# First transform of a long convolution by channel halves of one sequence

## Chip, core and metric

The kernel runs on one core of a Trainium2 chip. The core has a matrix engine (PE, TensorE), whose weight loads are shown apart (PEld), a vector engine (DVE), a scalar engine (ACT), GpSimd (POOL) and a queue engine (SP); each works through its own instructions in order and waits for the others by semaphores. The metric is the device time of one execution in microseconds; of several executions the median is taken.

## What is computed

The input is x (8 sequences of 5696 positions and 128 channels), a filter h (5696 positions, 128 channels), 64 pairs of mixing matrices and one channel matrix. The reference, cut to what matters:

```python
# long convolution, position-wise causal
Xf = np.fft.rfft(x, n=2 * S, axis=1)
Hf = np.fft.rfft(h, n=2 * S, axis=0)
x = np.fft.irfft(Xf * Hf[None], n=2 * S, axis=1)[:, :S, :]
# spectral mixing of the lowest 64 modes
X = np.fft.rfft(x, axis=1)
Yr = einsum('bmd,mde->bme', Xr, w_r) - einsum('bmd,mde->bme', Xi, w_i)
Yi = einsum('bmd,mde->bme', Xr, w_i) + einsum('bmd,mde->bme', Xi, w_r)
u = x + np.fft.irfft(Y, n=S, axis=1)
out = u + np.maximum(u @ w_ch, 0.0)
```

## The kernel before

A position is written as 64 q + p, with q from 0 to 88 and p from 0 to 63. The long transform is done in two steps by matrix products. The *first transform* runs over q: for one channel, PE takes the 89 rows of x as weights (two sequences of 64 positions p make 128 columns) and a table F of cosines and sines as the moving operand, 180 columns: 90 frequencies k, real and imaginary. The result has 128 partitions (sequence, p). The *second transform* runs over p with twiddle matrices M: for each k, two parts r and two sequences b, a matmul that is 64 rows deep over 128 channels, into two PSUM banks, one for each sequence.

The eight sequences are worked in four pairs. For each pair the stages are:

- *First transform*, 32 tiles of four channels (`a_tile`): four matmuls into two PSUM banks, then one evacuation of 720 columns to the buffer As (lines 477 to 479), by ACT or DVE. In the first pair a string `SHARE` says which; each tile waits for all eight pieces of x of both sequences (`XIN`).
- *Second transform* in 23 ticks of four frequencies (`tick`, `second`). Each tick's result is copied from PSUM by ACT (Xs) or taken from PSUM by DVE, multiplied with the filter's spectrum Hs on DVE (U, line 652), transformed by PE with two matrices (`Wc`), evacuated by ACT (Zs), written to a scratch tensor, and reduced to 64 modes (`modes`, PSUM bank 7). Tick 0 is special: its matmuls are cut by channels (`DA`, `DF`: 116 or 120, then the rest), so that the first part can run before the last tiles are evacuated; it has three products (`first_u`, line 623).

The last stage (from line 773 on) mixes the modes, transforms back and writes the output. The change leaves its instructions alone, apart from where some of its buffers lie.

*The opening.* All DMA requests on x go through POOL's queue, which casts to 16 bits on the way: first h (six requests), then x of the first pair into the buffer Xr (14 requests: for each quarter c of the positions `first_rows` of both sequences, `next_rows` for both together, and `last_row`), then the twiddle table M (six). Meanwhile PE runs 92 filler matmuls. Then h has its own first transform, 16 tiles, each of four matmuls and four fillers, evacuated by ACT except for two tiles. Between them, after every second tile, DVE copies one of the eight pieces of x (89 partitions, 2048 elements) to its place in the buffer Xin (`x_place`, line 365), in which each channel's step is 130 elements. Then PE runs 22 long fillers (`LONG`), and the 32 tiles of the first pair follow, with six *filter ticks* (`filter_tick`: the second transform of h, evacuated to Hs, then swapped between partition halves by two DMAs on SP) after tiles 11, 14, 17, 20, 23 and 26. The other filter ticks run in the second transform of the first pair, six ticks ahead of their use.

*The next pair's x* is requested on POOL's queue: for the second pair four pieces (buffers Xh, which lie in the part of Hs that is filled last, and where Xr lies before) right after the eight copies, and the other pieces in the ticks. DVE copies the pieces to Xin during the ticks named in `XPLACE`.

PSUM has eight banks. The tiles of the first pair and the filter ticks take turns at four slots of two banks (`FOUR`); the tiles of h at three.

A recorder keeps the order in which instructions are written down for each engine and adds the waits from the names of what is read and written (`("xin", i)`, `("as", j)`, `("h", t, 0)`, ...). Thus the order in the program is the order on each engine.

## Time and profile before

| | us |
|---|---|
| median of three runs | 371.91 |
| lowest, highest | 370.37, 372.64 |
| span of the profiled execution, first to last instruction | 370.1 |

The profiled execution's time outside its span is not given. Its granted PE clock was 0.999 of full speed over the whole span. Busy time by stretch, in microseconds of each stretch:

| stretch | what runs | PE | DVE | ACT | share of the DMA engines |
|---|---|---|---|---|---|
| 13.0 to 23.0 | first transform of h | 9.71 of 10 | 6.01 | 8.24 | 1.07 |
| 27.3 to 43.3 | first transform, first pair | 15.44 of 16 | 14.02 | 14.45 | 1.04 |
| 49.4 to 74.6 | second transform, first pair | 25.19 of 25.2 | 24.86 | 24.02 | 1.00 |
| 74.6 to 95.0 | its end, start of the next pair | 20.40 of 20.4 | 17.09 | 19.97 | 0.73 |

A matmul's end is modelled by the profiler, so PE looks busier than it is; a share of the DMA engines over 1 comes from transfers that overlap on one engine. In the profile, As is the result of the first transform, Ah that of h, F the table, Xin the placed x, Xr, Xh and Xt the pieces as they arrive, and L323 the one line by which all matmuls are issued (L320 all DMA requests; L311, L313, L315 and L317 all evacuations).

### The profile page before, as it was taken

The page shows a single profiled execution, that of the slowest core. Times are in us where ns is not written, and L with a number is a line of the kernel's source. Part 1 is how long each engine was busy: PE and PEld are TensorE (multiplying, and loading weights), DVE is VectorE, ACT ScalarE, POOL GpSimd, SP SyncE. Part 2 cuts the span into 40 slices and gives each one's busy share as a digit, 9 for nine tenths or more (in the row PEclk, how much of TensorE's full clock was granted, in tenths as well). Part 3 has the DMA queues.
Part 4 walks back from the last instruction along what each step waited for, and adds up shares of the span by engine and source line. Part 5 has one row for each costly group of instructions (what it writes and reads, how often), then busy time and mean ns, then how long its engine had stood idle before and what let it go on. Part 6 is the DMA issues. An engine that isn't in the chain of part 4 may idle for free.

```text
span 370.1 us, 12455 instructions
## 1 busy us (share of the span) xinstructions
PE 354.7 (96%) x5350; PEld 276.5 (75%) x5350; DVE 291.8 (79%) x332; ACT 316.2 (85%) x499; POOL 75.2 (20%) x117
## 2 busy tenths in 40 slices
PE   7999899999999999999999999999999999999994
PEld 7878766667866668866668766668899888888873
DVE  3549899988999999989999988775357777756666
ACT  8559999999999999999999999995467777688885
POOL 8804012100833311823213001151000000000000
PEclk9999999999999999999999999999999999999999
DMA  7999979969999996999996999999999999999878
GB/s 139 209 271 382 249 165 292 232 198 283 93 140 213 263 258 186 132 160 215 263 278 128 171 310 363 342 345 388 381 410 386 413 410 408 418 399 376 326 291 349
DMA packets 87048, 103.94 MB, mean 281 GB/s; under 512 B 22730, under 2 KB 72522, under 8 KB 83438
## 3 DMA queue, kind: packets, MB, share of 16 engines
q1 hardware_dynamic: 64610, 81.33, 62.5%
q0 software_dynamic: 22384, 21.83, 35.4%
q8 instruction: 42, 0.69, 0.7%
q14 instruction: 12, 0.10, 0.1%
HBM read 70.61 MB, written 51.12 MB: 329 GB/s over the span
## 4 chain that ended last, share of the span: by engine, by line
PE 78%; ACT 10%; DMA 7%; DVE 3%; issue 1%; POOL 1%; DVEq 0%; POOLq 0%
PE ps L323 78%; ACT As L313 6%; DMA out_dram<-O 5%; DMA Hin<-in_h_dram 2%; ACT R L898 1%; DVE As L317 1%; ACT Xs L311 1%; DVE U L623 1%; POOL Hin L320 1%; ACT UT L311 1%; DVE O L899 0%; ACT Zs L311 0%; DVE Hp L438 0%; ACT C L313 0%; DVE Hs L315 0%
## 5 line engine op out<-in xcount | busy, mean ns | idle before, releaser
L652 DVE TENSOR_TENSOR U<-Xs,Hs 128x2048 f16<-128x2048 f16 (+1 forms) x72 | 85.8, 1197 | 12.1 <-ACT Xs L311 11.5
L323 PE MATMUL ps<-U,Wc 128*128 128x512 f16 (+1 forms) x368 | 93.8, 376 | 1.4 <-DVE U L623 1.4
L311 ACT CAST Xs<-ps 128x1024 f16<-128x1024 f32 (+1 forms) x76 | 75.0, 995 | 5.8 <-PE ps L323 3.1
L311 ACT CAST Zs<-ps 128x512 f16<-128x512 f32 (+1 forms) x132 | 70.1, 605 | 0.7
L899 DVE TENSOR_TENSOR O<-ps,R 128x512 f32<-128x512 f32 x81 | 52.4, 684 | 21.6 <-ACT R L898 11.4
L898 ACT ACTIVATE R<-ps 128x512 f32<-128x512 f32 (+1 forms) x92 | 50.5, 592 | 8.5 <-PE ps L323 8.4
L317 DVE TENSOR_SCALAR As<-ps 128x720 f16<-128x720 f32 x64 | 53.1, 879 | 4.8 <-PE ps L323 3.3
L323 PE MATMUL ps<-As,M 64*128 64x128 f16 (+3 forms) x1504 | 52.5, 214 | 2.4 <-ACT As L313 1.2
L313 ACT ACTIVATE As<-ps 128x720 f16<-128x720 f32 (+1 forms) x68 | 48.2, 771 | 5.0 <-PE ps L323 4.8
L323 PE MATMUL ps<-F,Xin 128*128 128x180 f16 x512 | 52.1, 249 | 0.1
L323 PE MATMUL ps<-WI,UT 128*128 128x256 f16 x360 | 50.8, 278 | 0.5 <-ACT UT L311 0.4
L311 ACT CAST UT<-ps 128x712 f16<-128x712 f32 x46 | 34.5, 752 | 19.4 <-PE ps L323 18.4
L323 PEld LDWEIGHTS ps<-U,Wc 128*128 128x128 f16 x368 | 29.1, 97 | 28.2 <-DVE U L623 1.9
L323 PEld LDWEIGHTS ps<-F,Xin 128*128 128x128 f16 x512 | 45.2, 155 | 6.7 <-DVE Xin L365 0.9
L323 PEld LDWEIGHTS ps<-As,M 64*128 64x128 f16 x1504 | 42.2, 94 | 8.7 <-ACT Xs L311 1.9
L323 PEld LDWEIGHTS ps<-WI,UT 128*128 128x128 f16 x360 | 38.9, 152 | 3.2 <-issue 1.8
L323 PE MATMUL ps<-IBs,C 128*128 128x356 f16 x128 | 39.2, 314 | 0.8 <-DVE O L899 0.7
L320 POOL DMA_DIRECT2D Xt<-in_x_dram x40 | 21.4, 540 | 76.5 <-PE ps L323 76.0
L323 PEld LDWEIGHTS ps<-G,Zs 128*128 128x128 f16 x512 | 26.1, 96 | 14.1 <-ACT Zs L311 0.2
L652 DVE TENSOR_TENSOR U<-ps,Hs 128x2048 f16<-128x2048 f32 (+1 forms) x16 | 35.5, 2216 | 0.0
L323 PE MATMUL ps<-G,Zs 128*128 128x128 f16 (+2 forms) x512 | 31.9, 192 | 0.1
L311 ACT CAST Zt<-ps 128x512 f16<-128x512 f32 x52 | 29.1, 659 | 0.0
(76 smaller groups left out, 479.4 us busy)
## 6 DMA issues: line engine op xcount, KB each, us to landing
out_dram<-O SPq DMA_DIRECT2D x39, 512.0 KB, 10.5
zscr<-Zs SPq DMA_DIRECT2D x62, 256.0 KB, 6.7
zscr<-Zt SPq DMA_DIRECT2D x26, 256.0 KB, 6.6
Xt<-in_x_dram POOLq DMA_DIRECT2D x20, 320.0 KB, 6.9
W<-wscr SPq DMA_DIRECT2D x4, 1024.0 KB, 8.5
ZT0a<-zscr SPq DMA_DIRECT2D x4, 1024.0 KB, 11.0
M<-cM POOLq DMA_DIRECT2D x5, 720.0 KB, 17.6
ZT1a<-zscr SPq DMA_DIRECT2D x3, 1024.0 KB, 11.1
```

Source lines behind the costliest of these rows:

```text
L311: R.add(e, lambda h_: h_.copy(dst, src), reads, writes, after=after)
L313: R.add(e, lambda h_: h_.activation(dst, src, COPY, scale=scale), reads, writes, after=after)
L317: R.add(e, lambda h_: h_.tensor_scalar_mul(dst, src, scale), reads, writes, after=after)
L320: R.add(eng, lambda h_: h_.dma_start(dst, src), reads, writes, ring=ring, after=after)
L323: R.add("tensor", lambda h_: h_.matmul(o, l, r, start=st, stop=sp), reads, writes)
L623: R.add("vector", lambda e: e.tensor_tensor(bass.AP(u_s[0], b * 512 + d0, [[2048, P], [1024, 2], [D, n], [1, d1 - d0]]), bass.AP(s_[0], s_ ...
L652: R.add("vector", lambda e: e.tensor_tensor(uv, src, hv, MULT), bk + [("h", t, 0), ("h", t, 1, 0), ("h", t, 1, J)], [("u", i)])
L898: R.add("scalar", lambda e: e.activation(rv, src_r, RELU), bk, [("r", i % NR)], after=once(("r", i % NR), G_ALL + XTT + [("y", 0), ("y", 1 ...
L899: R.add("vector", lambda e: e.tensor_tensor(ov, src_u, rv, ADD), bk + [("r", i % NR)], [key + (h_,)], after=once(key, old))
```

## The change

- *Zero columns.* The sine columns of frequencies 0 and 89 are zero. They are left out: F has 178 columns (`NF`), every evacuation of a tile 712 instead of 720, and the second transform has one part instead of two for these two frequencies, in x and in h.
- *Channel halves of one sequence.* Xin is laid out by sequence and channel half. The weights of one matmul in the first transform are two channel halves (d and d + 64) of one sequence instead of one channel of two sequences. Tiles 0 to 15 belong to sequence 0 and 16 to 31 to sequence 1. In the first pair a tile waits only for the pieces of sequence 0, or from tile 16 on for those of sequence 1 as well. In the second transform the partition halves are channel halves, and 128 columns hold 64 channels of each of the two sequences. The layouts of Hs, U and Xs follow.
- *Tick 0* is cut by sequence: `second` for sequence 0 before the tick (it needs tiles 0 to 15), for sequence 1 in it, in banks of its own (4 and 5), with 64 columns each; two products instead of three.
- *The opening.* Requests of x go sequence by sequence, 12 instead of 14. In the transform of h only the four pieces of sequence 0 are copied, after every fourth tile; DVE evacuates six tiles instead of two; two fillers a tile instead of four, and four long ones instead of 22. The four pieces of sequence 1 are copied among the tiles of the first pair, after tiles 1 and 5 by GpSimd, after 8 and 11 by DVE. The filter ticks stand after tiles 19, 21, 23, 25, 27 and 29. The second pair's four first pieces are requested after tiles 18, 20, 23 and 26, once these are evacuated.
- `modes` waits for both evacuations of a tick's Zs, since each holds a channel half.

```diff
+    NF = 2 * NK - 2
-    f1 = np.zeros((P, 2 * NK))
+    f1 = np.zeros((P, NF))
...
-    def x_place(i, src, toks):
-        R.add("vector", lambda e: e.tensor_copy(bass.AP(x_sb, i * XN * XS, [[XW, NQ], [XS, XN], [1, D]]),
+    def x_place(i, src, toks, eng="vector"):
+        R.add(eng, lambda e: e.tensor_copy(bass.AP(x_sb, i // XC * 2 * XH + i % XC * XN * HS, [[XW, NQ], [HS, XN], [XH, 2], [1, DH]]),
                                                 src),
               list(toks) + XZ, [("xin", i)])
...
+    for b_ in range(2):
+        for c_ in range(XC):
+            first_rows(b_, c_)
+            if c_ == 0:
+                next_rows(b_)
+                last_row(b_)
...
-    ZSLOT, DA, DF = 6, 116, 120
+    ZSLOT = (6, 4)
...
-    WARM, LONG = 92, 22
+    WARM, LONG = 92, 4
...
-        for i in range(4 if j < 15 else 0):
+        for i in range(2 if j < 15 else 0):
...
-             eng="vector" if j in (3, 7) else "scalar")
-        if j % 2:
-            i = j // 2 % 2 * XC + j // 4
+             eng="vector" if j in (2, 4, 6, 9, 11, 14) else "scalar")
+        if j % 4 == 3:
+            i = j // 4
...
-    def a_tile(j, slots, eng=None):
+    def a_tile(j, slots, eng=None, first_pair=False):
+        b_ = j // 16
+        xin = XIN[b_ * XC:b_ * XC + XC] if first_pair else XIN
...
-               ap(x_sb, XW, 0, P, d, [[XS, 2 * J]]), f1_sb[:, :], True, True,
-               XIN + XZ + [("f1",)], [bank(t + i // 2)])
+               ap(x_sb, XW, 0, P, d // DH * 2 * XH + d % DH, [[HS, 2 * J]]), f1_sb[:, :], True, True,
+               xin + XZ + [("f1",)], [bank(t + i // 2)])
...
+    def second(g_, t, bs=(0, 1)):
+        sl = slot_of(g_, t) if t else ZSLOT[bs[0]]
+        rd = [("as", j) for j in range(16 * bs[0], 16 * bs[-1] + 16)] + [("as", 32)] * (bs[-1] == 1)
...
+            product(g_, t, (ps, sl[0], 4096), bk[0], (0,))
+            second(g_, 0, (1,))
+            evac(bass.AP(x_s[e], 256, [[1024, P], [512, 2], [1, n]]), pv(ZSLOT[1], 256, [[512, 2], [1, n]]), bk[1], [("xs", e)], eng="scalar")
+            product(g_, t, (x_s[e], 0, 1024), [("xs", e)], (1,))
...
-    for i in range(NXH):
-        x_load(1, i, x_h[i], xtok(i), [t_ for r_ in XR for t_ in r_])
+    XTICK = [1, 5, 8, 11]
+    XNEXT = [18, 20, 23, 26]
+    HTICK = [19, 21, 23, 25, 27, 29]
     for j in range(32):
-        a_tile(j, FOUR, "both" if j == 31 else SHARE[j])
-        if j >= 11 and j % 3 == 2 and (j - 11) // 3 < LH:
+        a_tile(j, FOUR, "both" if j == 31 else SHARE[j], True)
+        if j in HTICK:
             h_ = turns("s", FOUR)
-            filter_tick((j - 11) // 3, [h_, h_ + 1])
-    second(0, 0, 0, DF)
+            filter_tick(HTICK.index(j), [h_, h_ + 1])
+        if j in XNEXT:
+            e = XNEXT.index(j)
+            x_load(1, e, x_h[e], xtok(e), [("as", j)] + [t_ for r_ in XR for t_ in r_])
+        if j in XTICK:
+            i = XC + XTICK.index(j)
+            x_place(i, bass.AP(x_all, i * XB, [[RA, NQ], [D, XN], [DH, 2], [1, DH]]), XR[i], "gpsimd" if i < XC + 2 else V)
+    second(0, 0, (0,))
```

More of the change, by code (lines that the diff above doesn't have):

```diff
@@ L493, in filter_tick @@
         for i, k in enumerate(ticks[t]):
-            for r in range(2):
+            sk = slots(k)
+            for n_, slot in enumerate(sk):
+                r = (slot + 1) % 2 if k else 0
                 for dh in range(2):
@@ L508, in filter_tick @@
         for p0, p1 in ((0, J), (J, 0)):
[L509 to L511 removed]
+            dma("sync", bass.AP(h_sb, p0 * 2 * HW + lo + 2 * w, [[2 * HW, J], [1, 2 * w]]),
+                bass.AP(h_sb, p1 * 2 * HW + lo, [[2 * HW, J], [1, 2 * w]]), "s", [("h", t, 0)], [("h", t, 1, p0)])
+        if t in GTICK:
+            q_ = GTICK.index(t)
+            s0, s1 = q_ * GP, min(q_ * GP + GP, NS)
             dma("sync", g_sb[:, s0 * P:s1 * P], bass.AP(c_g, s0 * P, [[GW, P], [1, (s1 - s0) * P]]), "c", (),
[L513 removed]
+                [("g", q_)], after=[("ag", k) for k in range(s0, s1)])
     def load_w(i):
@@ L580, in bass_long_conv_fft__then__afno_spectral_mix_kernel @@
     LC, LM, LH = 2, 3, 6
+    GTICK = [2 * i + 1 for i in range(NG)]
     ZR = 96
@@ L602, in slot_of @@
     def slot_of(g_, t):
-        if t == 0:
-            return ZSLOT
         if g_ == 0:
@@ L621, in first_u @@
-    def first_u(b, s_, row, tok, d0, d1):
-        n = len(ticks[0])
-        R.add("vector", lambda e: e.tensor_tensor(
-            bass.AP(u_s[0], b * 512 + d0, [[2048, P], [1024, 2], [D, n], [1, d1 - d0]]),
-            bass.AP(s_[0], s_[1] + d0, [[row, P], [0, 2], [D, n], [1, d1 - d0]]),
-            bass.AP(h_sb, d0, [[2 * HW, P], [HW, 2], [D, n], [1, d1 - d0]]), MULT),
-              [tok, ("h", 0, 0), ("h", 0, 1, 0), ("h", 0, 1, J)], [("u", 0)])
+            sk = slots(k)
+            for n_, slot in enumerate(sk):
+                r = (slot + 1) % 2 if k else 0
+                for dh in range(2):
+                    col = k * 3 * J + (J if r == 0 else 0) + dh * J
+                    mm(pv(sl + dh, bs[0] * 256 + i * DH, [[256, nb], [1, DH]]),
+                       ap(m_sb, MW, J * dh, J, col, [[1, P]]),
+                       ap(a_sb, AW, J * dh, J, slot * D + bs[0] * DH, [[1, nb * DH]]), n_ == 0, n_ == len(sk) - 1,
+                       rd + mtok(k), [bank(sl + dh)])
```

148 lines of the change are left out of this document (61 added, 87 removed).

## The prediction

> **What bounds the kernel now.** I read the page first, then the chain of waits in order of time, then the timeline of the opening and of one change of pair, engine by engine. Columns of chain and timeline: start, length (us), engine, line, what is written from what, count, idle time before it.
>
> ```profile
> span 370.1 us, 12455 instructions
> PE 354.7 (96%) x5350; PEld 276.5 (75%) x5350; DVE 291.8 (79%) x332; ACT 316.2 (85%) x499; POOL 75.2 (20%) x117
> PE 78%; ACT 10%; DMA 7%; DVE 3%; issue 1%; POOL 1%; DVEq 0%; POOLq 0%
> ```
> ```profile
> 4.12 7.83 DMA Hin<-in_h_dram
> ...
> 13.27 3.96 PE ps L323 x48
> ...
> 45.72 3.61 PE ps L323 x63
> ...
> 49.37 25.23 PE ps L323 x529
> ...
> 95.26 7.47 ACT As L313 x11
> 102.73 0.05 issue
> 102.78 0.37 PE ps L323 x8
> ```
>
> The long middle pieces (49.37 and after) are PE without a gap, and the change leaves their matmuls as they are, but for four short ones (64 rows deep) in each pair. So its place is elsewhere: the opening, to about 43 us, and the three changes of pair, where ACT's evacuations of As end last and a short chain follows before PE runs on. The 96% says nothing here: part of PE's busy time in the opening is filler.
>
> ```profile
> 4.65 7.51 POOL L320 DMA_DIRECT2D Xr<-in_x_dram  x14
> 11.98 2.37 DVE L438 COPY Hp<-Hin 89x4096 f16<-89x4096 f16 x2 [6.71 <-DMA Hin<-in_h_dram]
> 12.12 1.21 POOL L320 DMA_DIRECT2D M<-cM  x1
> 13.84 2.10 ACT L313 ACTIVATE Ah<-ps 128x720 f16<-128x720 f32 x3 [4.00 <-PE ps L323]
> 15.69 0.69 DVE L365 COPY Xin<-Xr 89x2048 f16<-89x2048 f16 x1 [1.34 <-DMA Xr<-in_x_dram]
> 16.30 0.90 DVE L317 TENSOR_SCALAR Ah<-ps 128x720 f16<-128x720 f32 x1
> 17.12 1.28 DVE L365 COPY Xin<-Xr 89x2048 f16<-89x2048 f16 x2
> ...
> 23.22 4.27 PE L323 MATMUL ps<-Hp,F 128*128 128x344 f16 x22
> ...
> 26.33 0.69 DVE L365 COPY Xin<-Xr 89x2048 f16<-89x2048 f16 x1 [0.81 <-DMA Xr<-in_x_dram]
> ...
> 27.33 4.68 PE L323 MATMUL ps<-F,Xin 128*128 128x180 f16 x48
> 27.60 4.15 POOL L320 DMA_DIRECT2D Xh<-in_x_dram  x8 [10.58 <-DVE Xin L365]
> 27.84 6.24 DVE L317 TENSOR_SCALAR As<-ps 128x720 f16<-128x720 f32 x7 [0.82 <-PE ps L323]
> 28.15 4.25 ACT L313 ACTIVATE As<-ps 128x720 f16<-128x720 f32 x6 [3.67 <-PE ps L323]
> ...
> 31.95 0.41 PE L323 MATMUL ps<-Ah,M 64*128 64x64 f16 x16
> ```
>
> The reader is to see that the first matmul on x (27.33) stands behind the last of eight copies (26.33), and this behind the last x transfer. PE's 22 long fillers only cover that wait. The transfer of h ends at 4.12 + 7.83 = 11.95; x then takes until 26.33, 14.4 us for both sequences.
>
> **Step 1, the start of the first transform.** Now sequence 0 is requested first, and tiles 0 to 15 wait for its four copies alone. Half of 14.4 us puts its last byte at 19.2. Three other things have to end too. PE: a tile of h has six matmuls instead of eight, at 3.96/48 = 82 ns, so 16 tiles end at 13.27 + 7.9 = 21.2, and four long fillers (4.27/22 = 0.19 each) at 22.0. ACT: ten evacuations at 2.10/3 = 0.70 from 13.84 end at 20.8. DVE: its first, of tile 2, starts at 13.27 + 2 x 0.49 + 0.57 (the 0.57 is 13.84 less 13.27) = 14.8; six at 0.82 (16.30 to 17.12) and four copies at 0.64 (1.28/2) make 7.5, so 22.3, and 0.2 for waits on three PSUM slots gives 22.5. DVE ends last; the first matmul on x starts at 22.7 instead of 27.33: 4.6 earlier. Bounds: 22.0 (PE) and 23.5 (a microsecond of waits).
>
> **Step 2, the length of the first transform.** Two copies of sequence 1 now lie in DVE's queue among the tiles, two on GpSimd; six of the filter ticks move to the second half.
>
> ```profile
> 40.81 0.57 ACT L311 CAST Hs<-ps 128x512 f16<-128x512 f32 x1
> 41.27 1.96 ACT L313 ACTIVATE As<-ps 128x720 f16<-128x720 f32 x3
> ```
> Before, it runs from 27.33 to ACT's end at 41.27 + 1.96 = 43.23, 15.9 us. After: DVE's first evacuation comes 0.5 after the first matmul (27.84 less 27.33), at 23.2; six at 6.24/7 = 0.89 and two copies at 0.64 make 6.6: the last copy of sequence 1 ends at 29.8, and tile 16 cannot start before. From its evacuation at 30.3 ACT has eight at 4.25/6 = 0.70, half a tile (0.5) and five filter ticks at 0.47 (40.81 to 41.27): 8.5, ending at 38.8. Before, ACT had sixteen, a half and five, 14.1 us, in the 15.1 from 28.15 to 43.23, so 1.0 of waits; with those and 0.6 more, because ACT now has the heavy second half and the four PSUM slots tie it to DVE, the end is 40.4. Bounds 39.3 and 41.2. Gain at this point 2.8, not 4.6: the 1.8 between go into the two copies and the uneven halves.
>
> What else must be ready 2.8 earlier (the timeline, the DMA issues of 32 to 34.4 us with their time to landing, and what the trace tells of the tile Xh; L365's row has ns and the first and last start):
>
> ```profile
> 33.01 3.04 SPq L320 DMA_DIRECT2D Hs<-Hs  x4
> Hs<-Hs SPq DMA_DIRECT2D x2, 64.0 KB, 7.0
> L365 DVE COPY Xin<-Xh x4: 677/678/680, 49.2 to 61.6; 89x2048 f16<-89x2048 f16 x4
> DMA to landing us min/median/max: 10.9/12.3/15.1
> ```
> The swap of filter tick 0 was issued at 33.01; it now follows tile 19: ACT's 16, 18 and 19 from 30.3 and the tick's own 0.57 end near 33.0, and it lands with its second issue at 33.9 + 7.0 = 40.9, where the first product, next on DVE after its last tile, wants it at about 40. That delays a product of 1.2 us to 42.1, the second (0.7) to 42.8; PE does not ask for it before the next tick's matmuls, 45.72 less 2.8 = 42.9. Hidden, with 0.1 to spare; its bounds are 0 and 0.7. The next pair's x (Xh) was requested at 27.60 and first copied at 49.2. It is now requested from tile 18 on, behind both GpSimd copies on POOL's queue, about 32.3 to 38; at the median 12.3 the first lands at 45.1 for a use at 46.4, at the longest (15.1) 1.5 late, with DVE's products queued behind. I take 0.
>
> GpSimd's copies: the trace has none, so bounds.
>
> ```profile
> L540 POOL MEMSET ZT0b<- x1: 1794/1794/1794, 225.4 to 225.4; 32x2048 uint32 x1
> ```
> A write of 2048 elements takes it 1.8; a copy also reads, so 1.8 to twice that, 3.6; I take 2.2, nearest to the memset. Sequence 1's first piece is whole at 30 of x's 45 shares (each copy's 80 rows are 5, eight rows of a sequence 2, its last row a half), 11.95 + 9.6 = 21.6; two copies end at 26.0, or 28.8 at 3.6. Tile 16 waits for DVE until 29.8 anyway: cost nothing, and that is their cover. The Trainium skill (GPSIMD Engine Reference, 4.1 Engine selection) calls one-input work on GpSimd roughly line-rate, which agrees with the memset; no run here shows a copy.
>
> **Step 3, the changes of pair.**
>
> ```profile
> 102.45 1.11 DVE L623 TENSOR_TENSOR U<-ps,Hs 128x928 f16<-128x928 f32 x1
> 103.17 2.43 ACT L311 CAST Xs<-ps 128x512 f16<-128x512 f32 x3 [0.45 <-PE ps L323]
> 103.78 0.69 DVE L623 TENSOR_TENSOR U<-Xs,Hs 128x1024 f16<-128x1024 f16 x1 [0.22 <-ACT Xs L311]
> 104.58 0.26 DVE L623 TENSOR_TENSOR U<-ps,Hs 128x96 f16<-128x96 f32 x1
> 104.90 1.04 PE L323 MATMUL ps<-U,Wc 128*128 128x512 f16 x4 [0.46 <-DVE U L623]
> 110.01 1.01 ACT L311 CAST Xs<-ps 128x1024 f16<-128x1024 f32 x1 [0.24 <-PE ps L323]
> L652 DVE TENSOR_TENSOR U<-ps,Hs 128x1024 f16<-128x1024 f32 x1 | 1.2, 1218 | 0.0
> ```
> Before, PE waits for three products of tick 0; the third, of 12 leftover channels, ends at 104.85. The change makes two products by sequence. The first grows from 928 to 1024 elements (1.11 to 1.22), 102.45 to 103.7, still before ACT's copy (103.76); the second is the same 0.69; the third is gone. PE's matmuls ahead of ACT's copy go from 8 (0.37) to 14, and a run of 16 with 64 columns took 0.41 (at 31.95), so nothing there. PE thus starts at 104.5, 0.38 earlier. But ACT works on without a gap from 103.17 until it waits 0.24 at 110.01; if it sets the pace, only 0.24 is had. I take 0.3.
>
> ```profile
> L313 ACT ACTIVATE As<-ps 128x720 f16<-128x720 f32 x64 | 46.6, 787 | 5.0 <-PE ps L323 4.8
> L313 ACT ACTIVATE As<-ps 128x360 f16<-128x360 f32 x4 | 2.1, 518 | 0.0
> ```
> In the groups by shape (busy us, mean ns, idle time before): eight fewer elements in each evacuation: (787 - 518)/360 = 0.75 ns an element, 6 ns; ACT has some 14 in a change of pair, 0.1. Together 0.4 at each of three, 1.2. Inner runs of 64 instead of 128 in copies, evacuations and products cost nothing: the copies of h (2.37 for 2 x 4096) run at the rate of x's (0.69 for 2048) with runs of 32. The last tick of each pair saves two matmuls, 0.1 in all.
>
> **Sum.** 2.8 + 1.2 + 0.1 = 4.1 off the span of 370.1: 366.0. The profiled execution's own time is not given beside its span; the three runs shown go from 370.37 to 372.64, so it is at or below them. Taken off the median, 371.9 - 4.1 = 367.8. The ends of the terms (start 22.0 to 23.5, transform's end 39.3 to 41.2, changes of pair 0.24 to 0.5 each) give 366.5 to 369.2 for this case.
>
> **Rivals.** First, *GpSimd holds up DVE's copy.* At 12.12 a request on POOL took 1.21 while DVE copied from SBUF to SBUF; those of x took 7.51/14 = 0.54. So the two engines shut each other out. GpSimd's first copy can start at 21.6, DVE's fourth at about 21.9: if GpSimd is first, DVE waits until 23.8 and all moves 1.7 to 1.9, to 369.6. If x lands half a microsecond later than I reckon, DVE is first and it costs nothing. The Trainium skill has this as an exclusive lock (SBUF — State Buffer, Who interferes with whom): whoever starts first holds the shared ports for the whole instruction. The row agrees, in the one order that it shows; the rule speaks against this change.
>
> Second, slower: *GpSimd's copies gate tile 16.* With T each, sequence 1 is ready at 21.6 + 2T; beyond 29.8, so from T = 4.1, PE stalls with 16 tiles to go. The gain of 4.1 is used up at T = 6.2, 1% is lost at T = 8.0; T = 8.5 gives 367.8 + 8.8 = 376.6. For it: three-dimensional pattern, 89 partitions, an operation that the trace lacks. Against: the memset is four times faster.
>
> Third, *the gain is given back behind the transform*: swaps and Xh late (0.7 and 1.5), waits at their upper bound: 370.5. Transfers are dense there.
>
> Fourth, *more*: ACT without the extra waits and 0.5 at each change of pair: 366.3.
>
> **How the numbers follow.** Forecast 0.53, GpSimd first 0.13, GpSimd slow 0.10, given back 0.10, more 0.14. A change under 1% (3.7 us) cannot be told from none, so the line lies at 368.2, inside the forecast's own range: 0.35 of its 0.53 are below it. With 0.14 for more and 0.06 of the two middle rivals at half their price: faster 0.55. Slower by over 1% is 0.10, GpSimd's copies; the rest, 0.35, is within 1%. The range from 365.6 to 371.9 takes in the middle rivals and leaves out the slow GpSimd and a small rest below.
>
> **What would show it.** First matmul on x at 22.7 (21.6 to 23.5 right; 24 or later behind a long DVE copy: GpSimd was first). Tile 16 at about 29.8, released by DVE's copy and not by POOL; POOL's copies near 2.2. Last As of the first pair at 40.4. The first product waiting for a swap by less than 1. Two products instead of three at each change of pair, and PE 1.8 instead of 2.2 after the last As. A time over 372, or a first transform that ends after 42, would make the prediction wrong.

## The result, and the profile after

| | before | after |
|---|---|---|
| median of 22 runs each, same chip | 372.47 us | 373.88 us |
| lowest, highest | 370.37, 374.82 | 371.98, 377.97 |
| ratio after/before, 95% interval | | 1.0043, 1.0022 to 1.0063 |
| span of the profiled execution | 370.1 us | 373.5 us |
| its granted PE clock | 0.999 | 0.987 |

The change makes the kernel 0.4% slower; forecast was 367.8, 1.1% faster. Ratios leave out executions more than 1.5% above the fastest of their kernel (here one of after's 22); medians take in all. The profiled execution of after took 375.28 us, so 1.8 lie outside its span; in the runs below it is about as much, at most 2.0. It is 1.4 above the median, so what is late in its profile is somewhat later than usual.

The page of after, three lines: span, busy times, granted clock in 40 slices of 9.3 us.

```profile
span 373.5 us, 12293 instructions
...
PE 351.1 (94%) x5274; PEld 271.4 (73%) x5274; DVE 293.0 (78%) x330; ACT 313.1 (84%) x495; POOL 77.3 (21%) x117
...
PEclk9999969999999999999999999999999999999998
```

PE has 3.6 us less to do than before (351.1 against 354.7, part of it fillers), and yet the span is 3.4 longer: it waits more. The clock row has a 6 in the sixth slice, 46.7 to 56.0 us, where before had nines throughout.

The timeline of the opening first, all engines; start, length, engine, line, operation, what ended the idle time before:

```profile
22.60 5.03 PE L328 MATMUL ps<-F,Xin 128*128 128x178 f16 x52 [0.38 <-DVE Xin L370]
23.08 3.73 POOL L370 COPY Xin<-Xr 89x2048 f16<-89x2048 f16 x2 [7.86 <-DMA Xr<-in_x_dram]
...
28.89 0.68 DVE L370 COPY Xin<-Xr 89x2048 f16<-89x2048 f16 x1
```

and ACT's last evacuations of the first transform:

```profile
38.68 1.19 ACT L318 ACTIVATE As<-ps 128x712 f16<-128x712 f32 x2
```

Up to here the change does what it says. The first transform starts at 22.60 and ends at 39.87, 3.4 earlier than before (43.23). GpSimd's two copies take 1.87 each and end at 26.8, ahead of DVE's last at 29.57.

Then the timeline of DVE from 40, the products of ticks 0, 1 and 2:

```profile
41.11 1.23 DVE L637 TENSOR_TENSOR U<-ps,Hs 128x1024 f16<-128x1024 f32 x1 [1.62 <-DMA Hs<-Hs]
42.44 0.69 DVE L637 TENSOR_TENSOR U<-Xs,Hs 128x1024 f16<-128x1024 f16 x1
43.86 1.23 DVE L637 TENSOR_TENSOR U<-Xs,Hs 128x2048 f16<-128x2048 f16 x1 [0.73 <-DMA Hs<-Hs]
48.62 1.23 DVE L637 TENSOR_TENSOR U<-Xs,Hs 128x2048 f16<-128x2048 f16 x1 [3.53 <-DMA Hs<-Hs]
```

and of PE behind them:

```profile
48.25 0.48 PE L328 MATMUL ps<-G,Zs 128*128 128x128 f16 x8 [2.06 <-DMA G<-cG]
50.50 0.61 PE L328 MATMUL ps<-Ah,M 64*128 64x64 f16 x16 [1.77 <-DVE Hs L320]
```

All three ticks (0, 1 and 2) wait for their swap of Hs, 5.9 us in all, the third for 3.5; PE stands for G as well, 2.1. The DMA issues from 32 to 44 us say why (last column: median from issue to landing). After:

```profile
Xh<-in_x_dram POOLq DMA_DIRECT2D x4, 320.0 KB, 8.0
Hs<-Hs SPq DMA_DIRECT2D x12, 64.0 KB, 9.1
G<-cG SPq DMA_DIRECT2D x2, 256.0 KB, 11.3
```

Before:

```profile
Hs<-Hs SPq DMA_DIRECT2D x12, 64.0 KB, 7.6
G<-cG SPq DMA_DIRECT2D x2, 256.0 KB, 9.1
```

The same twelve swaps and two pieces of G are requested in this stretch in both kernels. What differs is the neighbours and the time of use. Timelines of POOL and SP in after, first and last request of Xh and first swaps:

```profile
32.64 2.23 POOL L325 DMA_DIRECT2D Xh<-in_x_dram  x4 [5.83 <-ACT As L318]
...
37.51 1.03 POOL L325 DMA_DIRECT2D Xh<-in_x_dram  x2 [1.04 <-ACT As L318]
```
```profile
33.24 2.46 SPq L325 DMA_DIRECT2D Hs<-Hs  x4
```

and the first product of before, in DVE's timeline:

```profile
43.43 1.16 DVE L623 TENSOR_TENSOR U<-ps,Hs 128x960 f16<-128x960 f32 x1 [0.29 <-PE ps L323]
```

Before, Xh was requested at 27.60, ahead of the swaps; after, from 32.64 to 38.54, among them. And before, the first swap was issued at 33.01 for a product at 43.43, 10.4 later; now it is issued at 33.24 and wanted at 39.5 (41.11 less 1.62), 6.3 later. Tick 0's two swaps land as before, after 6.5 and 7.2. It is tick 2's that got longer. They stand on SP's queue behind the first piece of G (issued at 35.75, landed at 48.11), and G stands beside Xh. The DMA issues of these two swaps (windows 37 to 37.4 of before, 36.8 to 37.4 of after), and tick 2's product in before:

```profile
Hs<-Hs SPq DMA_DIRECT2D x2, 64.0 KB, 9.6
Hs<-Hs SPq DMA_DIRECT2D x2, 64.0 KB, 11.8
47.42 1.23 DVE L652 TENSOR_TENSOR U<-Xs,Hs 128x2048 f16<-128x2048 f16 x1 [0.51 <-ACT Xs L311]
```

In before they had landed at 46.82, 0.6 us ahead of the product at 47.42: that was all the room there was. In after they land at 48.54 for a DVE that is ready at 45.09. In both kernels they land within 0.7 us of the last piece of Xh (46.35 and 47.85). So landing got later while the use got earlier.

What the stall costs is more than its own length. The windows of 5 us (busy times of PE, PEld, DVE, ACT, POOL, then granted clock, share of the DMA engines, GB/s):

```profile
45.00:50.00 5.00, 1.54 (x14) 0.65 (x12) 1.47 (x3) 2.17 (x4) 0.00 (x0) 0.96 0.70 203
50.00:55.00 5.00, 4.50 (x68) 3.01 (x70) 4.10 (x6) 2.14 (x3) 1.04 (x2) 0.50 0.88 173
```

PE was busy for 1.54 of 5 us, and in the next 5 the granted clock was 0.50. In windows of 1 us it is 0.50 from 49.6 to 56.4, for 6.8 us. The Trainium skill (TensorE: Matmul & The Clock Gate, Part 1) has the clock at half after an idle window of some 3.4 us until the array has been busy as long. These rows agree in kind, but PE's longest idle stretch here is 2.1 us, then 1.8 with 0.5 us of work between, so less than 3.4 us without a break was enough.

The chain of waits of after, the pieces behind the stall and the ends of As. The swap in its first row is tick 3's, on which DVE's next evacuation waited (to 48.96); it landed 0.4 us behind tick 2's:

```profile
38.26 10.70 DMA Hs<-Hs
...
50.50 48.13 PE ps L328 x824
98.66 7.42 ACT As L318 x11
...
151.89 7.41 ACT As L318 x11
```

The second pair's last As ends at 106.08; before it was 102.73. So the 3.4 us gained at 39.87 have become 3.3 lost: 6.7 us are gone in one stage, in this execution. The third pair's ends at 159.30, 53.2 later, where before took 53.0, and the fourth's 53.6 after that: copies wait 1.8 us for the next pairs' x (Xt), which before didn't.

### The profile page after: what moved, and what is told of

It is laid out like the page before. It is cut to its first block, busy times and chain, and to the rows that moved or that the text cites. A ratio compares the mean times of both kernels' runs of the same rounds, so it can differ in the third digit from the quotient of the medians.

```text
span 373.5 us, 12293 instructions
## 1 busy us (share of the span) xinstructions
PE 351.1 (94%) x5274; PEld 271.4 (73%) x5274; DVE 293.0 (78%) x330; ACT 313.1 (84%) x495; POOL 77.3 (21%) x117
## 4 chain that ended last, share of the span: by engine, by line
PE 71%; DMA 10%; ACT 9%; DVE 5%; issue 2%; POOL 1%; DVEq 0%; SPq 0%; POOLq 0%
PE ps L328 70%; ACT As L318 6%; DMA Xt<-in_x_dram 4%; DMA Hs<-Hs 3%; DMA Xr<-in_x_dram 3%; DVE As L322 2%; ACT R L905 1%; DVE U L637 1%; DVE Xin L370 1%; POOL Hin L325 1%; ACT Xs L316 0%; DVE Ah L322 0%; ACT Zs L316 0%; ACT UT L316 0%; DVE O L906 0%
## 5 line engine op out<-in xcount | busy, mean ns | idle before, releaser
L637 DVE TENSOR_TENSOR U<-Xs,Hs 128x2048 f16<-128x2048 f16 (+1 forms) x76 | 88.6, 1171 | 17.6 <-ACT Xs L316 12.1
L328 PE MATMUL ps<-U,Wc 128*128 128x512 f16 (+1 forms) x368 | 95.0, 380 | 2.1 <-DVE U L637 1.9
L316 ACT CAST Xs<-ps 128x1024 f16<-128x1024 f32 (+1 forms) x76 | 75.1, 995 | 12.3 <-PE ps L328 11.2
L322 DVE TENSOR_SCALAR As<-ps 128x712 f16<-128x712 f32 x64 | 52.7, 871 | 4.6 <-PE ps L328 3.2
L328 PE MATMUL ps<-F,Xin 128*128 128x178 f16 x512 | 52.0, 249 | 2.3 <-DVE Xin L370 1.2
L328 PE MATMUL ps<-As,M 64*128 64x128 f16 (+1 forms) x1480 | 51.1, 217 | 2.5 <-ACT As L318 2.4
L318 ACT ACTIVATE As<-ps 128x712 f16<-128x712 f32 (+1 forms) x68 | 47.7, 764 | 4.0 <-PE ps L328 3.9
L328 PEld LDWEIGHTS ps<-As,M 64*128 64x128 f16 x1480 | 41.2, 95 | 8.2 <-ACT As L318 2.9
L637 DVE TENSOR_TENSOR U<-ps,Hs 128x2048 f16<-128x2048 f32 (+1 forms) x20 | 40.3, 2016 | 1.6 <-DMA Hs<-Hs 1.6
```

Of the source, the lines that this page charges most:

```text
L316: R.add(e, lambda h_: h_.copy(dst, src), reads, writes, after=after)
L318: R.add(e, lambda h_: h_.activation(dst, src, COPY, scale=scale), reads, writes, after=after)
L322: R.add(e, lambda h_: h_.tensor_scalar_mul(dst, src, scale), reads, writes, after=after)
L328: R.add("tensor", lambda h_: h_.matmul(o, l, r, start=st, stop=sp), reads, writes)
L637: R.add("vector", lambda e: e.tensor_tensor(uv, sv, hv, MULT), bk + [("h", t, 0), ("h", t, 1, 0), ("h", t, 1, J)], [("u", i)])
```

## The experiments

Each of the four groups ran on one chip, with the kernel before beside it; ratios are to that. Theory A: the swaps and G share the DMA engines with whatever long transfer is under way, so it counts when they are requested and beside what. Theory B: the bytes of the opening are too many whatever their order. Theory C: the halved clock is most of the loss. The end of the second pair's As and the time from the first matmul on ZT0 (the last stage) to the end are read from each trace, so from one execution of each kernel: they carry that execution's luck. Fillers, more warm-up, and layout only with and without Xh have four executions each, the others 8 to 12.

| kernel | ratio, interval | last As of pair 2, us | last stage, us | matmuls |
|---|---|---|---|---|
| before | | 102.73 | 121.3 | 5350 |
| after | 1.0043, 1.0022 to 1.0063 | 106.08 | 120.7 | 5274 |
| ticks early | 0.9981, 0.9941 to 1.0022 | 102.05 | 120.5 | 5274 |
| fillers | 1.0107, 1.0031 to 1.0184 | 103.75 | 126.0 | 5324 |
| Xh later | 1.0052, 1.0020 to 1.0085 | 105.38 | 121.2 | 5274 |
| copies on DVE | 1.0041, 1.0001 to 1.0080 | 103.51 | 120.6 | 5274 |
| layout only | 1.0127, 1.0039 to 1.0215 | 105.03 | 125.3 | 5322 |
| ticks early, M late | 0.9982, 0.9953 to 1.0012 | 102.00 | 120.8 | 5274 |
| M late | 1.0026, 0.9987 to 1.0065 | 102.71 | 120.3 | 5274 |
| no Xh | 0.9933, 0.9900 to 0.9966 | 100.66 | 120.4 | 5274 |
| before, no Xh | 1.0006, 0.9974 to 1.0038 | 103.33 | 120.2 | 5350 |
| layout only, no Xh | 1.0135, 1.0084 to 1.0185 | 103.77 | 125.4 | 5322 |
| Xh early, M late | 0.9965, 0.9932 to 0.9998 | 101.23 | 120.9 | 5274 |
| more warm-up | 1.0146, 1.0073 to 1.0220 | 104.67 | 124.6 | 5322 |
| layout only, fewer | 1.0056, 1.0021 to 1.0092 | 107.24 | 120.9 | 5274 |
| ticks early, no Xh | 0.9921, 0.9883 to 0.9959 | 99.29 | 119.9 | 5274 |

### Which transfers are in the way (first group)

**Ticks early.** The six filter ticks stand earlier among the tiles, so their swaps are requested earlier.

```diff
-    HTICK = [19, 21, 23, 25, 27, 29]
+    HTICK = [14, 16, 18, 20, 23, 26]
```

> The changed kernel with the six filter ticks after tiles 14, 16, 18, 20, 23 and 26 instead of 19 to 29; nothing else. In the changed kernel the second transform of the first pair starts 3 us earlier than before, but products and modes then wait for DMAs: the swap of tick 3 lands 11 us after its request (48.96), the first piece of G 12.4 us after its own (48.2). Theory A (the swaps and G share the engines, transfer by transfer, with the long transfers of M and Xh, so what counts is how early they are requested and what lies beside them): requested some 2.5 us earlier and partly before Xh, they land 2 to 4 us earlier; the wait of products for swaps falls from 5.9 to under 2.5, and the time falls by 3 to 5, to about 370. Theory B (the bytes of the opening as such fill the DMA engines until 46 and nothing can land before): waits within 1 us of the changed kernel's, time 373 to 374. Theory C (the lost time is mostly the halved clock after the stall): the time falls only if the stall falls under some 2 us.

371.77 us, 0.9981. The second pair's As ends 4.0 earlier than in after and the clock stays at 1.00. The swaps take no less (10.2 in the median from 32 to 44 us), they are only asked for earlier, and later ones still hold DVE up, 4.3 us between 38 and 80: A had set under 2.5, and a time of about 370. Two rows of its chain show the changes of pair without a stall between:

```profile
147.66 7.44 ACT As L318 x11
...
200.36 7.43 ACT As L318 x11
```

Between the two ends lie 52.69 us. The same two rows of before:

```profile
148.23 7.49 ACT As L313 x11
...
201.22 7.52 ACT As L313 x11
```

53.02: the new layout gains 0.33 us a pair.

**Xh later.** The four transfers leave the first transform for the first ticks, and their copies move back.

```diff
-    XLATE = [3, 6, 9, 12]
+    XLATE = [5, 7, 9, 12]
+    XEARLY = [1, 2, 3, 4]
...
-    XPLACE = [3, 5, 7, 9, 11, 14, 17, 20], [9, 10, 13, 14, 17, 18, 20, 22]
+    XPLACE = [6, 8, 9, 11, 13, 15, 17, 20], [9, 10, 13, 14, 17, 18, 20, 22]
...
-    XNEXT = [18, 20, 23, 26]
+    XNEXT = []
```

> The changed kernel with the four Xh pieces requested in ticks 1 to 4 of the first pair's second transform instead of after tiles 18 to 26, and copied in ticks 6, 8, 9 and 11 instead of 3, 5, 7 and 9 (the pieces after them requested in ticks 5, 7, 9 and 12, copied in 13, 15, 17 and 20). Theory A (the swaps and G wait beside Xh): from 36 us on only swaps and G are under way, they land in 3 to 6 us instead of 8 to 12, PE does not stall, the clock stays at 1.00, and the time falls by 4 to 6, to 368 to 370. Theory B (bytes as such, M above all): swaps land at most 1 us earlier, time 373 to 374.

375.06 us, 1.0052: A's 368 to 370 is missed. The DMA issues from 32 to 44 us, without Xh beside them:

```profile
Hs<-Hs SPq DMA_DIRECT2D x12, 64.0 KB, 3.5
G<-cG SPq DMA_DIRECT2D x3, 256.0 KB, 3.2
```

The same swaps that took 9.1 land in 3.5, and G in 3.2 instead of 11.3. From 37 to 44 us after moves 396 packets of POOL's queue and 482 of SP's, with 82.6% and 23.4% of the engines' time; with no Xh (third group) it is 1003 packets of SP's. The Trainium skill (DMA: Bandwidth & Descriptors, Queues, rings and completion order) says that each DMA engine serves its queues in turn, packet by packet. The near equal counts beside such unequal shares agree with it. But the gain is not kept. DVE at 61, in its timeline:

```profile
61.13 1.23 DVE L637 TENSOR_TENSOR U<-Xs,Hs 128x2048 f16<-128x2048 f16 x1 [4.49 <-DMA Hs<-Hs]
```

Now the swaps of later ticks stand beside Xh, ACT waits 4.2 us for a write to the scratch tensor, and the clock falls to 0.55 from 60 to 65. The collision moved with Xh: A's mechanism, though not its gain.

**Fillers.** Fifty matmuls on a spare bank, ahead of the first that waits for G, keep PE busy through the stall.

```diff
-    WARM, LONG = 92, 4
+    WARM, LONG, FILL = 92, 4, 50
...
+        for i in range(FILL if (g_, s_) == (0, 0) else 0):
+            mm(pv(MB, 0, [[1, NF]]), f1_sb[:, 0:P], f1_sb[:, :], True, True, [("f1",)], [bank(MB)])
```

> The changed kernel with 50 filler matmuls of 178 columns on PE (about 4 us at full clock) ahead of the first modes, where PE stood idle 2.1 us for G and then 1.8 for DVE; they write a bank that is not in use yet. Nothing that is computed changes. Theory C (about half of what is lost after the stall is lost to the PE clock, granted at 0.50 from 50 to 55 us and 0.86 from 55 to 60): the clock stays at 1.00, the waits for the swaps stay as they are, and the time falls by 2 to 3 us, to 371. Theories A and B alone (the clock follows, but DVE and ACT would have set the pace after the stall anyway): within 0.7 of the changed kernel.

376.51 us, 1.0107. In the windows the clock holds:

```profile
45.00:50.00 5.00, 4.55 (x59) 3.90 (x54) 2.76 (x4) 2.46 (x4) 0.00 (x0) 1.00 0.71 205
```

but products still wait 5.2 us for swaps, and the second pair's As ends at 103.75. That is 4.5 later than where it ends with hardly a swap late (99.29, the last experiment), and the clock is full: the halved clock is not most of the loss (C falls). What it costs by itself isn't shown. 103.75 is 2.3 below after, but copies on DVE, whose median is after's, ends at 103.51; 6.8 us at half clock can cost half of that, 3.4, at most. And the kernel is slower than after: its last stage takes 126.0 us instead of 120.7. See the fourth group.

**Copies on DVE.** All four copies of sequence 1 on DVE.

```diff
-            x_place(i, bass.AP(x_all, i * XB, [[RA, NQ], [D, XN], [DH, 2], [1, DH]]), XR[i], "gpsimd" if i < XC + 2 else V)
+            x_place(i, bass.AP(x_all, i * XB, [[RA, NQ], [D, XN], [DH, 2], [1, DH]]), XR[i], V)
```

> The changed kernel with all four copies of sequence 1 on DVE, none on GpSimd. In the changed kernel GpSimd's two copies took 3.7 us together, ended at 26.8, and nothing waited for them. Two more copies of 0.6 each in DVE's first half move tile 16 and the end of the first transform by 1.2. If the end of the opening is set by DMAs that land (theories A and B), this is hidden for the most part: time within 0.6 of the changed kernel. If it is set by the engines, it is 1.2 slower.

373.96 us, 1.0041: no difference from after. Its first transform ends 0.9 later (40.79), hidden behind the late swaps; GpSimd's copies neither help nor harm as long as these are late.

### M, and the layout alone (second group)

**M late, with the ticks early and alone.** The last two of M's six pieces are requested in ticks 0 and 2 of the first pair.

```diff
-    for i in range(MP):
...
+    for i in range(MP - 2):
+        load_m(i)
...
+            if g_ == 0 and t in (0, 2):
+                load_m(MP - 2 + t // 2, [("u", t % NU)])
```

> The changed kernel with filter ticks after tiles 14 to 26 and, besides, the last two of six pieces of M requested in ticks 0 and 2 of the second transform (used from ticks 5 and 9 on) instead of in the opening: 1.4 MB less ahead of Xh and beside the first swaps. Theory A: Xh is through 3 us earlier, swaps 2 to 6 land in under 8 us, waits for swaps before 55 us under 1 (2.5 with early ticks alone), and the time falls by 1 to 2 against early ticks alone (371.8), to 370 to 371. Theory B (all bytes up to 60 us count, wherever they lie): the wait turns up later, at 50 to 60, and the time stays within 0.7 of 371.8.

> The changed kernel with only the last two pieces of M requested in ticks 0 and 2. Theory A: Xh ends 3 us earlier, the swaps of ticks 2 and 3 land 2 to 3 us earlier than 48.96, the wait for swaps falls from 5.9 to about 3 and the time to 371 to 372. Theory B: within 0.7 of the changed kernel.

371.08 us, 0.9982, with the ticks early; 373.78, 1.0026, alone. Alone one swap is still late by 2.6 and the clock falls to 0.82; the interval takes in both before and after. A gain from holding back M is not shown.

**Layout only.** Opening, fillers, order of copies and ticks and requests as before; layout, zero columns and tick 0 as after.

```diff
-    for b_ in range(2):
-        for c_ in range(XC):
+    for c_ in range(XC):
+        for b_ in range(2):
...
-    WARM, LONG = 92, 4
+    WARM, LONG = 92, 22
...
-    HTICK = [19, 21, 23, 25, 27, 29]
+    HTICK = [11, 14, 17, 20, 23, 26]
+    for i in range(NXH):
+        x_load(1, i, x_h[i], xtok(i), [t_ for r_ in XR for t_ in r_])
```

> The opening of the kernel before (x requested quarter by quarter, eight copies on DVE among h's tiles, 22 long and four fillers, the first pair's tiles waiting for all of x, filter ticks after tiles 11 to 26, Xh requested ahead of the tiles) with all the rest of the change: zero columns left out, channel halves, tick 0 cut by sequence. In four kernels with the changed rest, undisturbed periods from one change of pair to the next were 52.7 us against 53.0 before. If the rest is good by itself, this kernel gains 0.25 to 0.35 at each of three changes of pair and some 0.2 in the opening: 1.0 to 1.3 below the kernel before, ratio 0.997, with no wait of products for swaps and a clock as before. If the new layout of Hs itself makes swaps slow, waits for swaps appear here too and the time is at or above the kernel before.

377.63 us, 1.0127: a clear miss. The first transform ends at 44.5 instead of 43.23. Its chain of waits shows the way: a copy of x on DVE waits for its transfer until 19.60, the evacuation of a tile of h stands behind it (20.31), and what PE has to do ahead of the first matmul on x behind that (21.18). And the last stage takes 4.0 us longer, where the change has touched no instruction.

### Without Xh (third group)

**No Xh, in after, in before and in the layout alone.** These kernels leave the four transfers out; the copies read Ah in their place, so pair two's output is not the reference's. With the transfers goes the wait of the last filter ticks for their place.

```diff
-            x_load(1, e, x_h[e], xtok(e), [("as", j)] + [t_ for r_ in XR for t_ in r_])
...
+                    if g_ == 0 and i < NXH:
+                        x_place(i, bass.AP(ah_sb, 9408, [[HW, NQ], [D, XN], [DH, 2], [1, DH]]), AHT)
```

> The changed kernel without the four transfers of the second pair's first pieces (Xh, 1.4 MB at 32 to 45 us); the four copies of them are made in the same ticks, but read the same number of elements of Ah, so pair two's numbers are not the reference's. Theory A (the swaps, G and the scratch writes come late because Xh lies among them): swaps land in 2.4 to 5 us as in the kernel with Xh later, products wait less than 1 us for them between 38 and 80, the clock stays at 1.00, the first pair's second As end comes at 102.7 less 3.3 = 99.4, and the time is the predicted 367 to 369, 0.986 to 0.992 of before. Rival C (the new order makes waits of its own, DMAs or not): waits for products or Zs remain, time 371 to 374.

> The kernel before, without the same four transfers (its copies read Ah too). If before is bound by PE and ACT there, as its chain of waits says, nothing changes: 0.997 to 1.003 of before, second As end at 102.4 to 102.9. If the DMA engines, busy at a share of about 1.0 from 4 to 74 us, already bound it, it gains 2 to 4 us: 0.990 to 0.995.

> The new layout under the order and the opening of before (the kernel that came out at 1.0127), without the four transfers as well. If its excess came from late transfers in the first pair, it falls to 0.994 to 0.999 of before (the three changes of pair at 0.3 each). If the layout itself costs time, it stays above 1.005, and stretches between As ends are longer than 53.0 without a DMA in the chain.

After falls from 1.0043 to 0.9933, 369.73 us; before stays at 1.0006. The same 1.4 MB are taken from both: before did not feel them, after pays 1.1% or 4.1 us for them, and the two intervals of after don't meet. No product waits for a swap between 38 and 80 us, and the clock stays at 1.00. That settles the place, and B in its plain form falls: before carries the same bytes at no cost that shows. The swaps of before were slow as well, 7.6 us against 2.5 without Xh; there they had the time. 0.9933 is just above A's 0.986 to 0.992; the last experiment takes up the rest. The layout alone stays at 1.0135, so its excess is not Xh; its pairs now take 52.7 us each (As ends 103.77, 156.47, 209.13), with no product waiting for a swap, and the whole excess stands in the first transform and in the last stage.

**Xh early, M late.** The whole computation. Xh is requested at once behind DVE's last copy of sequence 1, ahead of the swaps that are wanted next; filter ticks early, two pieces of M late.

```diff
-        if j in XNEXT:
-            e = XNEXT.index(j)
-            x_load(1, e, x_h[e], xtok(e), [("as", j)] + [t_ for r_ in XR for t_ in r_])
...
+        if j == XTICK[-1] + 1:
+            for e in range(NXH):
+                x_load(1, e, x_h[e], xtok(e), [t_ for r_ in XR for t_ in r_])
```

> Whole computation. Filter ticks after tiles 14, 16, 18, 20, 23 and 26, the last two pieces of M requested in ticks 0 and 2, and Xh requested at once after the last copy of sequence 1 (about 30 us) instead of after tiles 18 to 26. Theory A: Xh lands by about 40, before the swaps that are wanted from 42 on are due, so fewer waits than the 2.3 of PE for Hs that the kernel with early ticks and late M shows: 368 to 370.5, 0.990 to 0.997 of before. Rival B (the engines are full until 74 us whatever the order, a transfer moved makes another late): 371 to 372.5, 0.997 to 1.001.

371.77 us, 0.9965 with 0.9932 to 0.9998: 0.8% below after, and just below before. From the kernel with ticks early and M late (0.9982) the time alone doesn't tell it, and it lies between the ranges of A and B; the waits do. There products waited 2.4 us for swaps (38 to 80); here, from 36 to 82, one line is left:

```profile
DVE U L640 <- DMA Hs<-Hs: 0.4, 1, 0.4
```

### The stall in the last stage, and the rest of the gain (fourth group)

Three kernels (fillers, layout only with and without Xh) lose 4.6 to 5.3 us against after in the last stage, and all three have 48 or 50 matmuls more than after. Their chain of waits has a gap on PE that names no releaser. After, none:

```profile
253.86 4.87 PE ps L328 x152
```

Fillers:

```profile
251.08 3.41 PE ps L328 x105
254.49 2.88 issue
257.37 1.88 PE ps L328 x47
```

Layout only, no Xh:

```profile
250.15 3.50 PE ps L328 x108
253.65 2.55 issue
256.20 2.57 PE ps L328 x44
```

The run of 152 matmuls breaks near its 105th in both, with no wait that the chain names, and the window behind it has a lower clock (this of the layout without Xh):

```profile
255.00:260.00 5.00, 3.58 (x60) 3.41 (x60) 0.83 (x2) 0.38 (x1) 0.00 (x0) 0.66 1.03 381
```

**More warm-up** takes after and gives it 48 matmuls more where PE has nothing else to do, ahead of the transform of h; **layout only, fewer** takes 48 away from the layout alone at the same place. The number of columns stays about the same; the diff is that of the first, and the second has 44 fillers of 356 columns.

```diff
-    WARM, LONG = 92, 4
+    WARM, LONG = 140, 4
...
-        mm(pv(6 + i % 2, 0, [[1, NF]]), f1_sb[:, 0:P], f1_sb[:, :], True, True, [("f1",)], [bank(6 + i % 2)])
+        mm(pv(6 + i % 2, 0, [[1, 117]]), f1_sb[:, 0:P], f1_sb[:, 0:117], True, True, [("f1",)], [bank(6 + i % 2)])
```

> The changed kernel with 140 fillers of 117 columns in place of the 92 of 178 ahead of the transform of h: 48 matmuls more on PE, about the same columns, so the opening should not move by more than 0.5 us. Theory F (PE's stall of 2 to 3 us at about 254, with no releaser, is set by how many instructions PE has had, since the three kernels that show it have 48 or 50 matmuls more than the changed one): the stall appears here too, the last segment from the end of the last Zs to the end grows from 122.6 to 126 or 127, and the time is 1.012 to 1.018 of before, against 1.0043 for the changed kernel. Rival (the stall belongs to the layout under the order of before, or to late transfers): no stall there, 1.001 to 1.008.

> The new layout under the order and the opening of before (1.0127), with 44 fillers of 356 columns in place of 92 of 178: PE has as many matmuls as in the changed kernel. Theory F: no stall at 254, last segment 122 to 123, the excess of 1.1 per cent goes, 0.996 to 1.004 of before. Rival: the stall and the excess stay, 1.008 or more.

With more warm-up: 377.42 us, 1.0146, and the chain has the gap:

```profile
251.75 3.47 PE ps L328 x107
255.22 2.09 issue
257.31 1.95 PE ps L328 x45
```

With fewer, 374.84 us, 1.0056, and it is gone:

```profile
254.70 4.86 PE ps L328 x152
```

Both as the count of instructions has it: 48 matmuls more or fewer, some 240 us earlier, make or unmake the gap. In time it is 1.0% on (intervals apart) and 0.7% off (the intervals of layout only and of fewer overlap, and 1.0056 lies outside the 0.996 to 1.004 that was expected).

The traces show what PE waits for. In all four kernels with the gap PE stops at the same place in its stream, after 3797 or 3798 matmuls and 3798 weight loads. Part 3 of the page has a queue called instruction, with 41 packets in every kernel of 5274 matmuls and 42 in every one with more. In all four a packet of 16 KB of this queue lands as PE stops or while it stands (at 255.6 in layout only, 254.9 without Xh, 256.1 with fillers, 255.9 with more warm-up), and PE goes on 1.2 to 1.4 us later. The row for the gap of the layout without Xh (DMA queues, 253.65 to 256.20):

```profile
q8 instruction: 1, 0.02, 2.3%
```

In after the packet lands at 258.4, when 3791 matmuls were begun and the short run is nearly through; in layout only, fewer at 259.5 (3794); in before at 250.8, early in the run. So, in four traces of four, PE stands for its next instructions where the short run reaches the end of what has been fetched, and fillers ahead only shift the run against that place. Why the packet comes no earlier isn't shown. The layout alone keeps 0.6%; its profiled run has late swaps in the first pair (As of pair 2 at 107.24), so it is no proof of a cost of the layout itself.

**Ticks early, no Xh.** Both causes of late swaps taken away.

```diff
-    HTICK = [19, 21, 23, 25, 27, 29]
+    HTICK = [14, 16, 18, 20, 23, 26]
...
-            x_load(1, e, x_h[e], xtok(e), [("as", j)] + [t_ for r_ in XR for t_ in r_])
```

> The changed kernel without the four transfers of Xh (its copies read Ah instead, so pair two's numbers are not the reference's) and with the filter ticks after tiles 14, 16, 18, 20, 23 and 26. Theory A: with neither the bulk transfer nor the short lead, no product waits for a swap, the second As end comes at 99.5 to 100.5 and the time is 0.987 to 0.992 of before, which is what the prediction added up to. Rival (the rest of the gain is lost to DVE and ACT in the ticks that carry a filter tick, whatever the transfers): second As end at 101 or later, 0.993 to 0.997.

369.23 us, 0.9921 with 0.9883 to 0.9959. Its DMA issues from 32 to 44 us, and chain:

```profile
Hs<-Hs SPq DMA_DIRECT2D x14, 64.0 KB, 3.7
G<-cG SPq DMA_DIRECT2D x3, 256.0 KB, 4.8
```
```profile
91.85 7.44 ACT As L318 x11
```

The second pair's As ends at 99.29, 3.4 earlier than before: the whole gain of the opening arrives, and one wait of 0.6 for a swap is left. The span is 366.1, but that execution took 367.94, 1.3 below its kernel's median. The median's ratio is 0.3% above the forecast's (367.8/371.9 = 0.989), inside the interval.

## Why the prediction was wrong

*Step 1* was right: 22.60 for 22.7, with DVE's last copy ending last.

*Step 2* was right in its first half. The copies of sequence 1 were done at 29.57 (29.8), the last As came at 39.87 (40.4), so the gain there was 3.4 and not 2.8. GpSimd's copies took 1.87 (2.2 taken, 1.8 to 3.6 bounded) and hid behind DVE's, as reckoned.

Its second half, "What else must be ready", is the step that failed: the overlap of the transfers with the first ticks, priced at "Hidden, with 0.1 to spare; its bounds are 0 and 0.7". Three things were wrong in it.

- Only the swap of tick 0 was followed. For it the 7.0 held (6.5 and 7.2); it landed at 41.07 (40.9 was said) and held its product up by 1.6, since DVE was ready at 39.5. The sum stopped there. Tick 2's swaps had landed 0.6 us ahead of their use in before, after 9.6; wanted 2.8 earlier, they would have been 2.2 late even if they had landed as before. They landed 1.7 later still (48.54), held the product up by 3.5, and PE with it. PE also stood 2.1 for G, which the step doesn't name.
- Xh was asked only for its own lateness. There "I take 0" held: its requests landed in 5.8 to 9.9 us instead of 12.3, and no copy waited for them. What it does to the small transfers beside it had no term, and that is what no Xh shows: 4.1 us.
- A stall of PE was priced at its length, while the clock behind it was at half for 6.8 us, which can cost 3.4 (half of it) at most.

*Step 3* was right in kind: two products at a change of pair, PE 1.92 after the last As (106.08 to 108.00) instead of 2.17:

```profile
107.17 0.69 DVE L637 TENSOR_TENSOR U<-Xs,Hs 128x1024 f16<-128x1024 f16 x1 [0.17 <-ACT Xs L316]
108.00 1.02 PE L328 MATMUL ps<-U,Wc 128*128 128x512 f16 x4 [0.60 <-DVE U L637]
```

0.25 where 0.3 was taken; a whole pair without a stall gains 0.33 where 0.4 was.

*The sum.* Of its 4.1, 3.0 are there by the medians when the transfers are on time (369.23 against 372.22 in the last experiment). That its profiled span meets the sum (366.1 for 366.0) is luck in good part: against before the opening gave 3.4 for 2.8, the next two pairs lost 0.9 (copies waited for Xt) where two changes of pair were to give 0.8, and the last stage, which the change leaves alone, was 1.2 shorter.

*The rivals.* Neither GpSimd rival came: its first copy started at 23.08, behind DVE's fourth, and both were done 2.8 before DVE's last. Whether the two engines shut each other out is not tested by it: their copies overlapped by 0.17 us. The third, "the gain is given back behind the transform", is what happened. It had the right place and the right transfers, the swaps ahead of Xh; its price of 2.7 (370.5 for 367.8, with 0.7 for the swap and 1.5 for Xh) was well under the 6.7 that the profile shows in one stage and the 6.1 between forecast and median, and its chance of 0.10 went with that price. Of its two terms the one for Xh never came. Its own sentence, "Transfers are dense there", was the reason to follow all six swaps, each from its landing in before to its use.

*Of the signs listed*, two failed: the first product waited 1.6 instead of under 1, and the time is over 372. The others came as said.

What stays open: how much of the 0.6% of the layout alone is more than late swaps and a late first transform, what the halved clock costs by itself, and why PE's instruction packet comes no earlier.

## What to carry to other kernels

When a change starts a stage earlier, list every transfer that the stage wants in its first ticks, with its issue, its landing and its use. The least room between landing and use, in the trace that you have, is what the stage can be moved before something waits; here it was 0.6 us. Don't take a landing from a trace in which other transfers were its neighbours: a small transfer beside a bulk one on another queue took up to three times as long here (7.6 against 2.5). What helped was to ask for the small transfers earlier, and, in the waits if not clearly in the time, for the bulk one ahead of them; to move it behind only moved the collision. When a kernel with a few more or fewer filler instructions changes its time at a place that it doesn't touch, compare the number of instructions before looking for a reason in the change.

## What the runs showed of the hardware that was not expected

- *PE can stand for its own instructions.* Four kernels with 5322 or 5324 matmuls have a gap of 1.2 to 2.9 us inside the same run of short matmuls (0.03 us each), at the same place in PE's stream, with a 16 KB instruction packet landing as PE stops or in the gap, and half clock for 3.4 us behind it. Their last stage takes 124.6 to 126.0 us; all with 5274, and before with 5350, have 119.9 to 121.3.
- *Swaps beside a bulk transfer.* 64 KB from partitions to partitions, requested from 32 to 44 us, take 2.3 to 3.7 us in the median without Xh under way, 7.6 to 10.2 with it; G's 256 KB 3.2 to 4.8 against 8.9 to 11.3.
- *The clock.* It stood at 0.50 for 6.8 us after one stretch of 5 us with PE busy for 1.54, and not at all where fillers made that 4.55. It can fall without a long idle stretch: in Xh early, M late it is at 0.50 for 3.4 us from 42.3 on, with PE busy for 4.00 of 5 us and idle for at most 0.5 at a time. Ticks early has the same 4.00 at a clock of 1.00. The row of the former:

```profile
40.00:45.00 5.00, 4.00 (x82) 2.20 (x74) 3.42 (x4) 4.03 (x6) 0.56 (x1) 0.73 1.05 275
```

- *GpSimd's copy* of 89 x 2048 elements of 16 bits took 1.87 us, DVE's 0.68.
